# Attention and two MLPs on one core: two token chunks share a pass of the MLPs, and the weights' spill is taken out

## The chip, the cores and the metric

The kernel runs on one core of a Trainium2 chip. The metric is the device time of one execution in microseconds (us); lower is better. TensorE (PE) multiplies, VectorE (DVE), ScalarE (ACT) and GpSimd (POOL) do the elementwise work, and SyncE (SP) issues every transfer.

## What is computed

The reference, cut to what matters. Attention over 2 batches, 8 heads, 576 positions and 64 dimensions a head, with a bias from relative positions that a small MLP makes, is followed by two MLPs over the 1152 tokens (512 to 2048 to 512): the first with ELU, the second with softplus.

```python
def _attn_ref(q, k, v, w1, b1, w2):
    scores = scale * np.matmul(q, k.transpose(0, 1, 3, 2))
    psi_rel = np.log1p(np.abs(rel))
    psi_i = np.log1p(np.maximum(pos[:, None], 1.0))
    h = np.maximum((psi_rel / psi_i)[..., None] @ w1 + b1, 0.0)
    scores = scores + (h @ w2).transpose(2, 0, 1)[None]
    attn = np.exp(scores - np.max(scores, axis=-1, keepdims=True))
    attn = attn / (np.sum(attn, axis=-1, keepdims=True) + 1e-09)
    return np.matmul(attn, v)

def _moe_ref(x, w_in, w_out):
    h = x @ w_in
    return np.where(h > 0.0, h, np.exp(np.minimum(h, 0.0)) - 1.0) @ w_out

def _moe2_ref(x, w_in, w_out):
    h = x @ w_in
    return (np.maximum(h, 0.0) + np.log1p(np.exp(-np.abs(h)))) @ w_out
```

## The kernel before

Everything is computed in split precision: an operand is a high part and a low part, and a product is three matmuls (high by high, high by low, low by high).

**Attention.** The queries stand in blocks (`BLOCKS`), the first of 64 rows of both batches together, the others of 128 rows; a unit is a block, a batch and a pair of heads, 36 in all. Ahead of a block its bias is made in stages of 16 rows (`bias_y`, `bias_mm`, `bias_ev`, `bias_out`): four `y` tiles on VectorE or GpSimd, two half-stages of 12 matmuls into `pb`, an eviction of each by ScalarE into `sg`, and a transfer that lays the rows out by head. A unit then has `scores` on TensorE, `soft` on VectorE (bias added, row maximum taken: `e` and `mx`), `expo` on ScalarE, `turn` (nine groups of four transposes for four units), `e_hi` and `e_lo` (tile `et`), and `av`, 30 matmuls with V. Four units end in 128 finished tokens (`fin_x`, `fin_t`, `fin_hi`, `fin_lo`), split into `xh` and `xl`, which the MLPs read. Before all this V needs a power-of-two scale from its largest entry: `v_bound` on ScalarE, `v_max` on VectorE, then `all_max` over the partitions (a diagonal by VectorE, a matmul with ones, a reduction by VectorE), in one piece.

**MLPs.** Tokens stand in chunks of 512, 256 and 384 (`CHS`). A weight tile `f`, of 16, has 128 of the 2048 hidden columns. For chunk `c` and tile `f` of layer `m`, `ffn1` forms the first product in one PSUM bank (12 matmuls), ScalarE and VectorE apply the activation (two or three ScalarE passes, then `both` on VectorE, the last that reads the bank), `hi` and `lo` split it into `g`, and `drain` multiplies by the second weights into accumulators that stay in four banks. Four banks hold first products. A chunk goes through all 16 tiles before the next begins, in the order of `ORDER`: 0, 1, 2 in the first layer and 0, 2, 1 in the second.

**Weights.** They arrive as 64-bit floats, in 64 halves of tiles (32 for each layer), and are built into 32-bit words on the core: a load of 512 KB (`dma`), a first pass on ScalarE (`abs`), a clamp on VectorE or GpSimd and three integer steps on VectorE (`bits`), then `split_hi` on ScalarE and `split_lo` on VectorE. The words of the first layer are made during the attention and the first MLP pass, written to device memory (`spill`) and read back ahead of their use (`reload`). Those of the second layer are made when their place in SBUF comes free.

**Order.** Every step is a task with an engine, a cost and a due time (`DUE`, `LEAD`); the class `Order` forms a list of each engine's instructions from them when the program is built, eight rounds forward and backward. Each engine then works in that order. Where the list has TensorE idle before the first `av`, `idle` puts warm-up matmuls on the identity into the gap:

```python
    def idle(at, gap):
        if not pas:
            warm(min(int(gap * 0.92 / 0.094), 60))
```

and 34 stand at the very start.

Of the kernel before, what the change touches and what calls it, by code (L numbers as in the profile page):

```python
# [27 lines left out]
CHS = [512, 256, 384]  # L28

ORDER = [(0, 1, 2), (0, 2, 1)]  # L30
# [18 lines left out]
NRAW, NWB, NRL = 2, 3, 3  # L49
# [5 lines left out]
    BY=-9.79, BMM=-1.13, BEV=-3.13, BOUT=15.84, VD=-7.95, VB=-11.68, VHI=1.98, VLO=33.24, VS=-9.83, VZ=-10.22,  # L55
    KH=12.0, KL=1.05, KB=5.39, QH=-0.25, QL=8.6, QD=14.51, SC=3.22, SO=-22.46, EX=2.92, EH=7.47, EL=-6.03,
    TR=-8.2, AV=5.84, FS=3.18, FX=16.16, FT=-19.73, FH=5.97, FL=12.76, TAB=18.07, WD=11.76, WA=4.33, WS=-6.11,
    WB=-4.29, RL=-1.33, WL1=7.35, AC=-5.72, GH=17.01, GL=-21.01, DR=-22.41, DH=11.55, FI=6.5, R1=0.61, R2=-1.7,
    WI=19.2, F1=56.11,
)  # L60
LEAD = [-1.26, 21.84, 8.41, 24.57, -1.58]
# [50 lines left out]
class Weights:  # L112
# [76 lines left out]
def attention(xctx, tc, qe, qt, kt, vt, par, tab, xh, xl, W, M):  # L189
# [82 lines left out]
    warm(34)  # L272
# [80 lines left out]
    def idle(at, gap):  # L353

        if not pas:
            warm(min(int(gap * 0.92 / 0.094), 60))
# [300 lines left out]
    vsx = add(V, 2.2, lambda e: (all_max(vg, vm[:, 0:1]), v_scale()), [vmx], -0.5)  # L657
# [128 lines left out]
    def weights(i, x):  # L786
# [3 lines left out]
        di = DUE["WD"] + DUE["WI"] * (2 * i + x) if m == 0 else dj - DUE["WL1"]  # L790
# [20 lines left out]
    def tile_of(j):  # L811
# [3 lines left out]
        if c == ORDER[m][0]:  # L815
# [19 lines left out]
        half = 2 * n <= 512  # L835
        if not half or f % 2 == 0:
            r_g.append(([hi], []))
        else:
            hi.order.append(t_hi[seq[j - 1]])
        g_use = r_g[-1][1]  # L840
        t_hi[t] = hi
# [235 lines left out]
class Mlps:  # L1077


    def __init__(self, ctx, tc, xh, xl, W, out):  # L1080
        self.ctx, self.tc, self.nc, self.xh, self.xl, self.W, self.out = ctx, tc, tc.nc, xh, xl, W, out
        self.gt, self.outs = [], {}

        self.ps4 = ctx.enter_context(tc.tile_pool(name="ps4", bufs=1, space=PSUM)).tile([P, 4, 512], F32, name="ps4")
        self.acc = [self.ps4[:, n] for n in range(4)]

    def open(self):
        self.ap = self.ctx.enter_context(self.tc.tile_pool(name="ap", bufs=2, side="right"))
        self.W.open_early()
# [158 lines left out]
```

## Time and profile before

| | us |
|---|---|
| median of three runs | 638.02 |
| lowest and highest | 634.76, 638.15 |
| the profiled execution | 637.52 |
| its span, first to last instruction | 635.7 |
| TensorE busy (5427 matmuls) | 610.2 |
| VectorE, ScalarE, GpSimd busy | 432.2, 406.8, 129.6 |
| granted TensorE clock, mean | 0.985 |

The busy time of TensorE counts matmuls that overlap, so it is an upper bound. The other rows are averages over three stages with different limits: a start of some 56 us, the attention up to about 220 us, and the MLPs. A line number in a row is that of the program printed above; a row's names are the program's, with buffer numbers left out. In the trace a group of instructions in a row stands as one line, with its count behind the x.

### The profile page before, as it was taken

The numbers are of one execution on the slowest core, as the hardware profiler recorded it, in microseconds if no ns is written. First come the engines' busy times: TensorE is split into PE (matmuls) and PEld (weight loads), VectorE is DVE, ScalarE is ACT, GpSimd is POOL, SyncE is SP. The second block draws the span as 40 slices with busy tenths as digits, with TensorE's granted clock in tenths as the row PEclk, the third lists the DMA queues.
The fourth block names the chain that finished last, engine by engine and source line by source line (L and its number), as shares of the span: only waits on it lengthen the run. The fifth ranks groups of instructions, "written<-read, shape, count | busy, mean of one in ns | idle before, by whom it ended". The sixth has DMA issues, their size and how long they took to land.

```text
span 635.7 us, 13697 instructions
## 1 busy us (share of the span) xinstructions
PE 610.2 (96%) x5427; PEld 520.8 (82%) x5427; DVE 432.2 (68%) x857; ACT 406.8 (64%) x831; POOL 129.6 (20%) x172
## 2 busy tenths in 40 slices
PE   6889989898999999999999999999999999999996
PEld 5667767676777888888899999998888889988985
DVE  4669888898799998887742248879788732223322
ACT  3644779899899985665553345659577554445652
POOL 5212768876661000000000001110010100000000
PEclk8879999999899999999999999999999999999999
DMA  8625454646254377887400003333333210000000
GB/s 329 208 84 163 138 149 143 189 137 166 72 157 155 88 208 236 269 254 222 157 27 1 1 0 100 122 121 123 125 108 114 86 47 20 1 1 18 34 1 33
DMA packets 28288, 73.21 MB, mean 115 GB/s; under 512 B 3136, under 2 KB 3520, under 8 KB 27968
## 3 DMA queue, kind: packets, MB, share of 16 engines
q1 hardware_dynamic: 28224, 72.34, 36.7%
q8 instruction: 42, 0.69, 0.5%
q14 instruction: 22, 0.18, 0.1%
HBM read 49.79 MB, written 10.75 MB: 95 GB/s over the span
## 4 chain that ended last, share of the span: by engine, by line
PE 84%; DVE 5%; ACT 4%; DMA 3%; POOL 1%; issue 1%; DVEq 0%; POOLq 0%; ACTq 0%
PE ps L1158 32%; PE ph L1118 31%; PE warm L270 6%; PE pb L387 4%; PE tp L550 4%; PE ps L510 4%; PE pa L575 3%; DMA bias<-sg 2%; ACT e L537 1%; DVE e L520 1%; ACT sg L399 1%; POOL y L378 1%; DVE et L559 1%; ACT et L554 1%; DMA sp<-sg 1%
## 5 line engine op out<-in xcount | busy, mean ns | idle before, releaser
L1118 PE MATMUL ph<-xh,wh 128*128 128x512 f32 (+2 forms) x384 | 130.0, 338 | 0.7 <-DVE t L1134 0.7
L1118 PE MATMUL ph<-xl,wh 128*128 128x512 f32 (+2 forms) x384 | 129.5, 337 | 0.0
L1118 PE MATMUL ph<-xh,wl 128*128 128x512 f32 (+2 forms) x384 | 129.5, 337 | 0.0
L378 POOL TENSOR_SCALAR y<-tpk,nbp 128x576 f32<-128x576 f32 x108 | 90.7, 855 | 57.0 <-PE pb L387 54.3
L1158 PE MATMUL ps<-g,wh 128*128 128x512 f32 (+2 forms) x384 | 96.3, 338 | 0.0
L1158 PE MATMUL ps<-wh,g 128*128 128x512 f32 x288 | 92.1, 393 | 0.0
L154 POOL TENSOR_SCALAR w<-w 128x512 f32<-128x512 f32 x38 | 25.2, 663 | 299.6 <-ACT w L146 267.3
L1143 DVE TENSOR_TENSOR g<-t,g 128x512 fp32r<-128x512 f32 (+2 forms) x96 | 52.5, 555 | 39.4 <-ACT g L1140 37.4
L1118 PEld LDWEIGHTS ph<-xh,wh 128*128 128x128 f32 x384 | 72.3, 188 | 6.6 <-DVE t L1134 0.8
L1140 ACT CAST g<-t 128x512 fp32r<-128x512 f32 (+2 forms) x96 | 48.0, 508 | 46.3 <-PE ps L1158 35.4
L1118 PEld LDWEIGHTS ph<-xl,wh 128*128 128x128 f32 x384 | 72.5, 189 | 5.7
L1118 PEld LDWEIGHTS ph<-xh,wl 128*128 128x128 f32 x384 | 72.2, 188 | 5.5
L1158 PEld LDWEIGHTS ps<-g,wh 128*128 128x128 f32 x384 | 67.0, 188 | 5.4
L1136 DVE SCALAR_TENSOR_TENSOR t<-ph,t 128x512 f32<-128x512 f32 (+2 forms) x48 | 26.7, 557 | 61.6 <-ACT t L1130 61.6
L1158 PE MATMUL ps<-g,wl 128*128 128x512 f32 (+2 forms) x192 | 64.6, 336 | 0.0
L1158 PEld LDWEIGHTS ps<-wh,g 128*128 128x128 f32 x288 | 54.1, 188 | 12.1
L399 ACT ACTIVATE sg<-pb,bcst,inv 128x288 f32<-128x288 f32 x72 | 42.5, 590 | 30.8 <-PE pb L387 27.6
L559 DVE SCALAR_TENSOR_TENSOR et<-tp,et 128x512 f16<-128x512 f32 x81 | 53.8, 682 | 6.2 <-ACT et L554 6.1
L1158 PE MATMUL ps<-wl,g 128*128 128x512 f32 x144 | 56.7, 394 | 0.0
L146 ACT ACTIVATE w<-r 128x512 f32<-128x512 f32 x64 | 42.7, 669 | 21.6 <-DMA r<-in_wb_dram 10.7
L537 ACT ACTIVATE e<-e,mx 128x576 f32<-128x576 f32 x72 | 55.6, 774 | 1.4 <-DVE mx L520 1.4
L550 PE MATMUL tp<-ident,e 128*128 128x128 f32 x324 | 49.7, 284 | 4.4 <-DVE xl L615 2.9
(116 smaller groups left out, 1069.6 us busy)
## 6 DMA issues: line engine op xcount, KB each, us to landing
r<-in_wa_dram SPq DMA_DIRECT2D x32, 512.0 KB, 4.3
r<-in_wb_dram SPq DMA_DIRECT2D x32, 512.0 KB, 3.6
bias<-sg SPq DMA_DIRECT2D x32, 288.0 KB, 3.4
wd<-w SPq DMA_DIRECT2D x32, 256.0 KB, 4.5
rl<-wd SPq DMA_DIRECT2D x32, 256.0 KB, 4.3
kr<-in_kt_dram SPq DMA_DIRECT2D x4, 576.0 KB, 6.7
vr<-in_vt_dram SPq DMA_DIRECT2D x2, 1152.0 KB, 10.6
sp<-sg SPq DMA_DIRECT2D x8, 288.0 KB, 3.4
```

The costliest lines, as they stand in the source:

```text
L146: self.nc.scalar.activation(w.bitcast(F32), self.raws[i, x][:, :, 1].bitcast(F32), AF.Abs)
L270: nc.tensor.matmul(wdst, wi[:, :P], wi[:, : 512 - SH], start=True, stop=True)
L378: eng.tensor_scalar(y, tpk[:, b0 : b0 + S], BIG, nbp[:, qd : qd + 1], op0=ALU.min, op1=ALU.max)
L399: nc.scalar.activation(sgs[bi, s][:, n * SH : (n + 1) * SH], pbs.pop((bi, s, n)), AF.Identity, bias=bcst, scale=inv[:, col : col + 1])
L537: nc.scalar.activation(e, e, AF.Exp, bias=mxs[u][:, x : x + 1], scale=-1.0, accum_out=sums[u - hp][:, h : h + 1])
L550: nc.tensor.transpose(tp[:, r], e[:, t * P : (t + 1) * P], ident)
L559: nc.vector.scalar_tensor_tensor(et[:, 1], tp, 2.0**14, et[:, 0], op0=ALU.mult, op1=ALU.subtract)
L1118: nc.tensor.matmul(ps, a[:, kk], x[:, kk], start=n == 0, stop=n == 3 * KT - 1)
L1136: nc.vector.scalar_tensor_tensor(t[0], ps, 0.0, t[0], op0=ALU.max, op1=ALU.add)
L1140: nc.scalar.copy(g[0], t[0])
L1143: nc.vector.tensor_sub(g[1], t[0], g[0])
L1158: self.nc.tensor.matmul(o, a, x, start=f == 0 and n == 0, stop=f == FT - 1 and n == 2)
```

## The change

1. `ORDER` is replaced by `PASSES`: chunks 0 and 1, 768 tokens, go through the weight tiles together, and chunk 2 follows. In the first layer chunk 1 trails by four tiles (`LAG`). A weight tile so serves 768 tokens in the first pass.
2. Chunk 1 has accumulators of its own in two banks (`ps2`), so two banks hold first products, one on each side. In the first layer two 256-column accumulators share a bank, which a matmul with a zero tile opens. The `g` tiles of chunk 1 are a pair of buffers of their own.
3. `spill` and `reload` are gone. The weights of the first layer go from load to split in one run, like those of the second; there are three buffers for raw words and four for words, instead of two, three and three for reloads.
4. `all_max` gives way after the diagonal and after the matmul, so that other instructions can stand between; the scale of V becomes three tasks.
5. Warm-ups: 22 at the very start instead of 34; in a gap half of what is left after 1 us, at most 20. The program has 101 instead of 357.
6. The due times and the choice of engine for each `y` tile, clamp and cast are new, so every engine's order changes.

```diff
-ORDER = [(0, 1, 2), (0, 2, 1)]
+PASSES = [(0, 1), (2,)]
+
+LAG = [4, 0]
...
-NRAW, NWB, NRL = 2, 3, 3
+NRAW, NWB = 3, 4
...
-    WI=19.2, F1=56.11,
+    WB=4.81, WL1=14.9, AC=1.55, GH=8.27, GL=-8.52, DR=9.09, FI=-0.31, R1=-0.34, R2=0.5, F1=32.77,
...
-    def spill(self, i, x):
-        self.nc.sync.dma_start(self.dram[i][x], self.words.pop((i, x)))
-
-    def reload(self, i, x):
-        w = self.words[i, x] = self.rl.tile([P, DM], F32, tag="rl", name=f"rl{i}{x}")
-        self.nc.sync.dma_start(w, self.dram[i][x])
...
-    warm(34)
+    warm(22)
...
         nc.vector.tensor_scalar_mul(dg, ident, src)
+        yield
         pm = pst.tile([P, 512], F32, tag="pt", name=f"pm_{dst.name}")[:, :P]
         nc.tensor.matmul(pm, ones, dg, start=True, stop=True)
+        yield
         nc.vector.tensor_reduce(dst, pm, axis=mybir.AxisListType.X, op=ALU.max)
...
-            warm(min(int(gap * 0.92 / 0.094), 60))
+            warm(min(int(max(gap - 1.0, 0.0) * 0.5 / 0.094), 20))
...
-    vsx = add(V, 2.2, lambda e: (all_max(vg, vm[:, 0:1]), v_scale()), [vmx], -0.5)
+    vsx = add(V, 0.29, lambda e: next(vmax), [vmx], -1)
+    vsx = vmm = add(T, 0.5, lambda e: next(vmax), [vsx], -1)
+    vsx = add(V, 1.0, lambda e: v_scale(), [vsx], -1)
+    r_pt.append(([vmm], [vsx]))
...
-    seq = [(m, c, f) for m in range(2) for c in ORDER[m] for f in range(FT)]
+    seq = []
+    for m in range(2):
+        for cs in PASSES:
+            for f in range(FT + LAG[m] * (len(cs) - 1)):
+                seq += [(m, c, f - LAG[m] * i) for i, c in enumerate(cs) if 0 <= f - LAG[m] * i < FT]
...
-        if m == 0:
-            sp = add(D_, 1.2, lambda e: W.spill(i, x), [a], di + DUE["WB"], lat=2.4)
-            r_word.append(([a0], [sp]))
-            a = rl = add(D_, 1.0, lambda e: W.reload(i, x), [sp, t_w], dj - DUE["RL"], lat=1.8)
...
+        self.zero = self.ap.tile([P, P], F32R, name="zero", bufs=1)
...
-        self.left = self.ctx.enter_context(self.tc.tile_pool(name="phleft", bufs=3, space=PSUM))
+        self.left = self.ctx.enter_context(self.tc.tile_pool(name="phleft", bufs=1, space=PSUM))
+        self.ps2 = self.left.tile([P, 2, 512], F32, name="ps2")
...
-        return 0 if j < NE else (j - NE + 1) % 4
+        return 0 if j < NE else (j - NE + 1) % 2
+
+    def acc(self, m, c, k):
+
+        if c != 1:
+            return self.ps4[:, k, : CHS[c] if m == 0 else DM]
+        return self.ps2[:, k // 2, k % 2 * CHS[c] :][:, : CHS[c]] if m == 0 else self.ps2[:, k]
...
+        tag, n, bufs = ("gs", CHS[1], 2) if c == 1 else ("g", 512, 3)
+        return [self.ap.tile([P, n], F32R, tag=f"{tag}{x}", name=f"g{x}{m}{c}{f}", bufs=bufs)[:, : CHS[c]] for x in range(2)]
...
+            two = m == 0 and c == 1
+            if two and f == 0 and j % 2 == 0:
+                self.nc.tensor.matmul(self.ps2[:, j // 2], self.zero, self.xh[0][:, 0], start=True, stop=False)
```

VectorE at the maximum of V. Before; `dg_vg` is the diagonal, `pm_vg` the result of the matmul, `vg` the maximum:

```order
L453 TENSOR_TENSOR vm<-vm 128x2
L454 TENSOR_TENSOR vm<-vm 128x1
L435 TENSOR_TENSOR q_522<-qr_0_248,q_521 128x256
L287 TENSOR_SCALAR dg_vg_535<-ident,vm 128x128
L290 TENSOR_REDUCE vg<-pm_vg_537 128x1
L276 TENSOR_SCALAR e_244<-vg 128x1
```

After:

```order
L448 TENSOR_TENSOR vm<-vm 128x2
L449 TENSOR_TENSOR vm<-vm 128x1
L430 TENSOR_TENSOR q_396<-qr_0_202,q_395 128x256
L277 TENSOR_SCALAR dg_vg_411<-ident,vm 128x128
L430 TENSOR_TENSOR q_403<-qr_1_205,q_402 128x256 x2
L151 TENSOR_SCALAR w_409<-w_409 128x512
L282 TENSOR_REDUCE vg<-pm_vg_436 128x1
L266 TENSOR_SCALAR e_198<-vg 128x1
```

Between the diagonal and the reduction now stand two subtractions of q parts and the clamp of a weight half.

VectorE in the attention, in the third and fourth block. Before; lines 156 to 160 are the integer steps on a weight half `w` from the raw words `r`, `e` and `mx` the softmax pass, `et` the low part of the transposed exponentials:

```order
L615 TENSOR_TENSOR xl_1010<-pr_4104,xh_1009 128x4x128
L559 SCALAR_TENSOR_TENSOR et_4_4136<-tp_4_4116,et_4_4136 128x512
L156 TENSOR_SCALAR w_3886<-w_3886 128x512
L435 TENSOR_TENSOR q_4102<-qr_1_3456,q_4101 128x256
L158 SCALAR_TENSOR_TENSOR w_3886<-r_3775,w_3886 128x512
L586 TENSOR_SCALAR sm_3794<-sm_3794 128x8
L160 SCALAR_TENSOR_TENSOR w_3886<-r_3775,w_3886 128x512
L559 SCALAR_TENSOR_TENSOR et_5_4204<-tp_5_4159,et_5_4204 128x512
L559 SCALAR_TENSOR_TENSOR et_6_4207<-tp_6_4166,et_6_4207 128x512
L520 ISA e_4261,mx_4260<-ps_98,bias_3335 128x576
L520 ISA mx_4260 128x1
```

After, at the corresponding place:

```order
L587 RECIPROCAL sm_3004<-sm_3004 128x8
L430 TENSOR_TENSOR q_3321<-qr_0_2737,q_3320 128x256
L518 ISA e_3592,mx_3591<-ps_64,bias_2123 128x576
L518 ISA mx_3591 128x1
L518 ISA e_3592,mx_3591<-ps_64,bias_2123 128x576
L518 ISA mx_3591 128x1
L557 SCALAR_TENSOR_TENSOR et_0_3594<-tp_0_3577,et_0_3594 128x512
L557 SCALAR_TENSOR_TENSOR et_1_3610<-tp_1_3584,et_1_3610 128x512
L591 SCALAR_TENSOR_TENSOR xs_3695<-pa_3404,xsc,sm_3004 128x512
L557 SCALAR_TENSOR_TENSOR et_2_3709<-tp_2_3697,et_2_3709 128x512
L557 SCALAR_TENSOR_TENSOR et_3_3724<-tp_3_3704,et_3_3724 128x512
```

The weight steps no longer stand between the passes of the attention.

VectorE in the first layer's first pass of the MLPs. Before; `t` and `g` are a tile's activation and its low part, `wl` a weight's low part from the reloaded words `rl`:

```order
L1143 TENSOR_TENSOR g_5619<-t_5591,g_5618 128x512
L154 TENSOR_SCALAR w_5625<-w_5625 128x512
L156 TENSOR_SCALAR w_5625<-w_5625 128x512
L158 SCALAR_TENSOR_TENSOR w_5625<-r_5577,w_5625 128x512
L160 SCALAR_TENSOR_TENSOR w_5625<-r_5577,w_5625 128x512
L1134 SCALAR_TENSOR_TENSOR t_5642<-t_5642,ph_5600 128x512
L1143 TENSOR_TENSOR g_5667<-t_5642,g_5666 128x512
L1134 SCALAR_TENSOR_TENSOR t_5671<-t_5671,ph_5629 128x512
L154 TENSOR_SCALAR w_5675<-w_5675 128x512
L156 TENSOR_SCALAR w_5675<-w_5675 128x512
L186 TENSOR_TENSOR wl_5615<-rl_5647,wh_5614 128x512
L1143 TENSOR_TENSOR g_5694<-t_5671,g_5693 128x512
```

After:

```order
L1132 SCALAR_TENSOR_TENSOR t_5073<-t_5073,ph_5029 128x512
L1141 TENSOR_TENSOR g_5047<-t_5021,g_5046 128x256
L157 SCALAR_TENSOR_TENSOR w_5042<-r_4971,w_5042 128x512
L155 SCALAR_TENSOR_TENSOR w_5056<-r_5003,w_5056 128x512
L1132 SCALAR_TENSOR_TENSOR t_5097<-t_5097,ph_5059 128x256
L157 SCALAR_TENSOR_TENSOR w_5056<-r_5003,w_5056 128x512
L1141 TENSOR_TENSOR g_5094<-t_5073,g_5093 128x512
L176 TENSOR_TENSOR wl_4974<-w_4944,wh_4973 128x512
L176 TENSOR_TENSOR wl_5123<-w_5056,wh_5122 128x512
L176 TENSOR_TENSOR wl_5053<-w_5042,wh_5052 128x512
L153 TENSOR_SCALAR w_5127<-w_5127 128x512
L1132 SCALAR_TENSOR_TENSOR t_5144<-t_5144,ph_5105 128x512
```

Passes of 512 and of 256 tokens alternate, and the weight steps stand between them.

## Rows read from the trace of the kernel before

**Rows 1.** Windows: length; busy us PE, PEld, DVE, ACT, POOL; clock; DMA; GB/s.

```profile
0.00:56.00 56.00, 46.15 (x461) 36.89 (x461) 36.72 (x84) 26.18 (x43) 15.56 (x26) 0.88 0.61 204
56.00:88.00 32.00, 30.80 (x613) 22.56 (x610) 27.79 (x53) 21.50 (x45) 19.61 (x23) 1.00 0.50 147
88.00:220.00 132.00, 123.26 (x2057) 95.85 (x2052) 120.37 (x263) 122.13 (x271) 78.25 (x100) 0.99 0.48 138
220.00:632.00 412.00, 409.96 (x2308) 365.46 (x2306) 246.92 (x460) 237.02 (x474) 16.19 (x24) 1.00 0.30 93
```

**Rows 2.** The page, part 4: the chain of waits, shares by line.

```profile
PE ps L1158 32%; PE ph L1118 31%; PE warm L270 6%; PE pb L387 4%; PE tp L550 4%; PE ps L510 4%; PE pa L575 3%; DMA bias<-sg 2%; ACT e L537 1%; DVE e L520 1%; ACT sg L399 1%; POOL y L378 1%; DVE et L559 1%; ACT et L554 1%; DMA sp<-sg 1%
```

**Rows 3.** The chain in order of time (start, length, what): DMA.

```profile
82.22 4.79 DMA sp<-sg
...
115.23 5.78 DMA bias<-sg
```

**Rows 4.** The same: matmul groups of attention and MLPs.

```profile
101.29 1.02 PE tp L550 x8
...
106.46 0.87 PE pa L575 x30
...
241.41 2.75 PE ph L1118 x12
...
274.38 2.80 PE ph L1118 x12
...
333.63 1.43 PE ph L1118 x12
```

**Rows 5.** Timeline of TensorE (start, length, what, idle before), first 44 us.

```profile
15.01 2.42 PE L270 MATMUL warm<-ident 128*128 128x224 f16 x12
...
34.52 0.80 PE L289 MATMUL pm_vg<-dg_vg,ones 128*128 128x128 f32 x2 [4.91 <-DVE dg_vg L287]
...
35.10 8.22 PE L270 MATMUL warm<-ident 128*128 128x224 f16 x60
...
43.26 0.44 PE L387 MATMUL pb<-y,w2h 128*32 128x288 f16 x8
```

**Rows 6.** Timeline of VectorE, first 57 us.

```profile
32.64 1.81 DVE L287 TENSOR_SCALAR dg_vg<-ident,vm 128x128 f32<-128x128 f32 x1
...
35.35 0.29 DVE L290 TENSOR_REDUCE vg<-pm_vg 128x1 f32<-128x128 f32 x1 [0.89 <-PE pm_vg L289]
...
43.85 1.81 DVE L380 TENSOR_SCALAR y<-tpk,nbp 128x576 f32<-128x576 f32 x4 [4.99 <-PE pb L387]
...
55.90 0.74 DVE L520 CUSTOM_DVE_ANT_0 e<-ps,bias 128x576 f32<-128x576 f32 x1
```

**Rows 7.** A 4 us window, columns as in rows 1.

```profile
36.00:40.00 4.00, 4.00 (x24) 3.27 (x23) 2.79 (x10) 3.44 (x5) 0.00 (x0) 0.52 0.27 73
```

**Rows 8.** Groups by shape: busy us, mean ns, idle before, releasers.

```profile
L156 DVE TENSOR_SCALAR w<-w 128x512 int32<-128x512 int32 x64 | 27.6, 432 | 9.2 <-POOL w L154 8.5
...
L158 DVE SCALAR_TENSOR_TENSOR w<-r,w 128x512 int32<-128x512 int32 x64 | 45.0, 703 | 1.1
...
L160 DVE SCALAR_TENSOR_TENSOR w<-r,w 128x512 int32<-128x512 int32 x64 | 46.6, 729 | 0.9
...
L146 ACT ACTIVATE w<-r 128x512 f32<-128x512 f32 x64 | 42.7, 669 | 21.6 <-DMA r<-in_wb_dram 10.7 <-DMA r<-in_wa_dram 10.6 <-DMA bias<-sg 0.3
...
L1125 ACT ACTIVATE t<-ph 128x512 f32<-128x512 f32 x16 | 9.6, 597 | 16.2 <-PE ph L1118 16.1
...
L1126 ACT ACTIVATE t<-t 128x512 f32<-128x512 f32 x16 | 10.1, 633 | 0.5
...
L1134 DVE SCALAR_TENSOR_TENSOR t<-t,ph 128x512 f32<-128x512 f32 x16 | 11.0, 685 | 4.6 <-ACT t L1126 4.5
```

**Rows 9.** Timeline of VectorE, two weight steps back to back.

```profile
220.39 0.68 DVE L186 TENSOR_TENSOR wl<-rl,wh 128x512 fp32r<-128x512 f32 x1
220.99 0.68 DVE L158 SCALAR_TENSOR_TENSOR w<-r,w 128x512 int32<-128x512 int32 x1
```

More of the change, by code (lines that the diff above doesn't have):

```diff
@@ L789, in weights @@
         dj = DUE["F1"] + w_first[m, f] + 0.4 * x
-        di = DUE["WD"] + DUE["WI"] * (2 * i + x) if m == 0 else dj - DUE["WL1"]
+        di = dj - DUE["WL1" if m else "WL0"]
         dw = add(D_, 1.9, lambda e: W.dma(i, x), [], di, lat=1.4)
@@ L834, in tile_of @@
         r_t.append(([ac], [hi, lo]))
[L835 to L841, printed above, removed]
         dr = t_dr[t] = add(
             T, 12 * (n / 2400 + 0.0155) if m == 0 else n / P * 3 * 0.231, lambda e: M.drain((m, c, f), made.pop(j)[4]), [hi, lo] + t_wp[m, f][1],
-            d + DUE["DH" if half else "DR"] * w,
+            d + DUE["DR"],
         )
-        g_use.append(dr)
+        r_gs[c == 1].append(([hi], [dr]))
         if j:
@@ L851, in tile_of @@
         if f == 0:
-            dr.after += t_acc
+            dr.after += t_acc[c == 1]
         if f == FT - 1:
-            t_acc.clear()
             fins = []
@@ L1081, in __init__ @@
         self.ctx, self.tc, self.nc, self.xh, self.xl, self.W, self.out = ctx, tc, tc.nc, xh, xl, W, out
-        self.gt, self.outs = [], {}
+        self.outs = {}
         self.ps4 = ctx.enter_context(tc.tile_pool(name="ps4", bufs=1, space=PSUM)).tile([P, 4, 512], F32, name="ps4")
-        self.acc = [self.ps4[:, n] for n in range(4)]
     def open(self):
         self.ap = self.ctx.enter_context(self.tc.tile_pool(name="ap", bufs=2, side="right"))
+        self.zero = self.ap.tile([P, P], F32R, name="zero", bufs=1)
+        nc = self.nc
+        nc.gpsimd.tensor_scalar(self.zero, self.xh[0][:, 0, :P].bitcast(F32), 0.0, 0.0, op0=ALU.mult, op1=ALU.mult)
         self.W.open_early()
@@ L1098, in slot @@
     def slot(self, j):
-        return 0 if j < NE else (j - NE + 1) % 4
+        return 0 if j < NE else (j - NE + 1) % 2
[3 more added lines that the diff above has]
+        return self.ps2[:, k // 2, k % 2 * CHS[c] :][:, : CHS[c]] if m == 0 else self.ps2[:, k]
     def g_tiles(self, m, c, f):
-        half = f % 2 if 2 * CHS[c] <= 512 else 0
-        if not half:
-            self.gt = [self.ap.tile([P, 512], F32R, tag=f"g{x}", name=f"g{x}{m}{c}{f}", bufs=3) for x in range(2)]
-        return [t[:, half * CHS[c] : (half + 1) * CHS[c]] for t in self.gt]
+        tag, n, bufs = ("gs", CHS[1], 2) if c == 1 else ("g", 512, 3)
+        return [self.ap.tile([P, n], F32R, tag=f"{tag}{x}", name=f"g{x}{m}{c}{f}", bufs=bufs)[:, : CHS[c]] for x in range(2)]
     def ffn1(self, m, c, f, slot):
@@ L1153, in drain @@
             if m == 0:
-                prods = [(self.acc[j][:, : CHS[c]], a[:, js], x) for a, x in ((h, gh), (h, gl), (l, gh))]
+                prods = [(a[:, js], x) for a, x in ((h, gh), (h, gl), (l, gh))]
             else:
-                prods = [(self.acc[j], a[:, js], x) for a, x in ((gh, h), (gh, l), (gl, h))]
-            for n, (o, a, x) in enumerate(prods):
-                self.nc.tensor.matmul(o, a, x, start=f == 0 and n == 0, stop=f == FT - 1 and n == 2)
+                prods = [(a[:, js], x) for a, x in ((gh, h), (gh, l), (gl, h))]
+            two = m == 0 and c == 1
+            if two and f == 0 and j % 2 == 0:
+                self.nc.tensor.matmul(self.ps2[:, j // 2], self.zero, self.xh[0][:, 0], start=True, stop=False)
+            for n, (a, x) in enumerate(prods):
+                self.nc.tensor.matmul(
+                    self.acc(m, c, j), a, x, start=f == 0 and n == 0 and not two, stop=f == FT - 1 and n == 2 and not (two and j % 2 == 0)
+                )
     def finish_hi(self, c, k):
-        self.nc.scalar.copy(self.xh[c][:, k], self.acc[k][:, : CHS[c]])
+        self.nc.scalar.copy(self.xh[c][:, k], self.acc(0, c, k))
     def finish_lo(self, c, k):
-        self.nc.vector.tensor_sub(self.xl[c][:, k], self.acc[k][:, : CHS[c]], self.xh[c][:, k])
+        self.nc.vector.tensor_sub(self.xl[c][:, k], self.acc(0, c, k), self.xh[c][:, k])
     def out_half(self, c, k, x):
@@ L1170, in out_half @@
         if x == 0:
-            self.nc.scalar.copy(o[:, sl], self.acc[k][:, sl])
+            self.nc.scalar.copy(o[:, sl], self.acc(1, c, k)[:, sl])
         else:
-            self.nc.vector.tensor_copy(o[:, sl], self.acc[k][:, sl])
+            self.nc.vector.tensor_copy(o[:, sl], self.acc(1, c, k)[:, sl])
     def out_dma(self, c, k):
```

54 lines of the change are left out of this document (27 added, 27 removed).

## The prediction, made before the changed kernel was run

> **What bounds the kernel now.** I read the stages first. From 220 us to 632 us TensorE is busy for 410 of 412 us, while VectorE and ScalarE have 247 and 237 [rows 1]. That is the two MLPs, and there only fewer matmul columns would help; the change keeps the columns. So what can be won lies before 220 us, and what can be lost lies in the MLPs becoming less dense. In the 132 us before 220, TensorE shows 123, VectorE 120 and ScalarE 122 us [rows 1]: three engines at over 90%, none alone the bound. In the first 56 us VectorE is busy for only 37 [rows 1]. The chain of waits puts 6% of the span, about 38 us, on warm-up matmuls [rows 2], more than on any single step of the attention. All of them stand before the first attention times V product, so nearly the whole start is blamed on matmuls whose results nobody reads. Last I looked for transfers on the chain: three waits like the two of 4.8 and 5.8 us shown, each for the last bias rows of a new query block [rows 3].
>
> **The profiled time.** Its span is 635.7 us, its time 637.5; the median of the three runs is 638.0. I sum against 637.5 and take 638.0 as its equal. Under 0.5%, some 3 us, a measurement can't be told from no change.
>
> **The start, up to the first softmax pass on VectorE, at 55.9 us [rows 6].** Three edits act here. (1) The cross-partition maximum of V is taken apart. Before, VectorE ran the diagonal (1.81 us from 32.64), then stood 0.9 us for the matmul and reduced at 35.35 [rows 6]; now a subtraction and a weight step fill that wait. This saves 0.9 us at most. (2) Sixty warm-ups stood behind that matmul and took 8.22 us, so the bias matmuls that follow began at 43.26 [rows 5], and VectorE stood idle for 4.99 us until they had freed its y buffers [rows 6]. Now 20 stand there. At the same 0.137 us each they take 2.7 us, which is 5.5 us less; the idle time goes, since its y work comes 5.5 us sooner than it waited. The planner asked for those sixty because it assumed 0.094 us for each. (3) Of the first 14 y tiles VectorE now makes all, before seven; four take it 1.81 us [rows 6]. And the 12 warm-ups that held the second half of bias stage 0 back from 15.01 to 17.4 [rows 5] no longer stand there. VectorE's own work up to the first softmax pass keeps its size (84 instructions before, 85 now), so what is won is idle time, of which there are 56 minus 37, or 19 us [rows 1]. About 5 us are bound to the loads and to the first chain and stay. Of the other 14 I take 10: the 5.0 and 0.9 above, and 4 of the first 30 us. The bounds: 13 us if every wait goes, 2 us if the clock (below) eats the rest.
>
> **The weights leave the attention.** By the built order VectorE had, between the first softmax pass and the first MLP tile, 2 clamps, 14, 13 and 13 of the three integer steps and 8 low-part subtractions; now 5, 4, 4, 4 and 3. That is 10 × 0.432 + 9 × 0.703 + 9 × 0.729 + 5 × 0.68 − 3 × 0.44 = 19.3 us of durations [rows 8, 9] (the clamp taken like the first step). Two steps in a row start 0.60 apart where each lasts 0.68 [rows 9], so it is 19.3 × 0.88 = 17 us of engine time. Against it stand 7 more y tiles, 7 × 0.45 = 3.2 us [rows 6], and 7 more q parts, about 2.5 us as an estimate from the same rows. VectorE is 11 us lighter for the same attention. ScalarE loses 9 of 13 first passes (0.669 each [rows 8]), 4 of 9 casts and 4 q casts, together about 9 us. Besides, the first MLP tile now stands some 3 us of TensorE's attention work earlier (five groups of 30 V products and 36 transposes follow it, before four and 20: 0.87 + 16 × 0.127 = 2.9 us [rows 4]); that only moves. TensorE itself loses warm-ups between 56 and 70 us and nothing else. Where three engines are equally full, the least relieved sets the gain: ScalarE's 9 us plus 2 of the moved work is my 11. The bounds: 3 us, if TensorE is the true bound there and only the moved work counts; 16, if the spills' and weights' transfers were also what made the bias waits 4.8 and 5.8 us [rows 3]. The spill and reload, 64 issues on SP, lie beside other work; I cost them at nothing else. The 32 loads of 512 KB of the first layer move with the weights: eight go before the last bias rows, the others in the first MLP pass, 1 MB for each 8.5 us of TensorE, or some 120 GB/s where the start had 204 [rows 1]. GpSimd's clamps now stand behind its last y tile and wait for nothing there.
>
> **The MLPs.** The matmul columns are the same; two zero matmuls of 512 columns are added (under 0.5 us). What the first pass costs VectorE: a weight tile now serves 512 + 256 tokens, so TensorE spends 2 × 2.80 + 2 × 1.43 = 8.5 us on it [rows 4]. VectorE needs for it two halves of 0.432 + 0.703 + 0.729 + 0.68 and two passes of 0.685 for the 512 tokens, some 0.42 each for the 256: (5.09 + 2.2) × 0.88 = 6.4 us [rows 8, 9], three quarters of TensorE's time. Before, a tile served 512 tokens in 5.6 us, for which VectorE would need (5.09 + 1.37) × 0.88 = 5.7: without work done ahead and spilled it could not keep up. With a cover of 8.5 us it can. What gets tighter is PSUM: the second chunk's accumulators take two banks, so two banks instead of four hold first products. A bank of 512 tokens is held for 0.597 + 0.633 on ScalarE and 0.685 on VectorE, 1.9 us plus hand-overs [rows 8], and between two uses stand a drain and a 256-token tile, 2.80 + 1.43 = 4.2 us [rows 4]. That leaves some 2 us for queueing; behind a first product that waits for its bank stand the drains, which have nothing to wait for, so a wait there is lost. I take 3 us of stalls for both layers, most of them among the first five tiles, where transposes, weight steps and MLP passes share VectorE; bounds 0 and 22. The 2.9 us of attention moved behind the first tile come back here. The last chunk is now 384 tokens, three output blocks to copy out instead of two: 0.4 us, between 0 and one VectorE pass of 0.74 [rows 6].
>
> **Sum.** 637.5 − 10 − 11 + 2.9 + 3 + 0.4 = 622.8, so 623 us.
>
> **Rivals.** (a) The clock. In the window from 36 to 40 us the granted clock was 0.52, that is mostly 1.2 GHz, after TensorE had stood idle for 4.91 us before the maximum's matmul at 34.52; from 56 us on it was 1.00 [rows 1, 5, 7]. With 101 warm-ups instead of 357 the start may run at 1.2 GHz throughout. A bias half-stage takes 0.44 us for eight of its twelve matmuls at 2.4 GHz [rows 5], some 0.5 in all, and would take 0.5 more; nine of them before the first softmax pass and some seven after it make 8 us, and the time would be 631. Against it: VectorE, not TensorE, is the fuller one there once the warm-ups go. The Trainium skill (TensorE: Matmul & The Clock Gate, What's actually happening) says that the throttled clock is the default and that activity releases it, which speaks against cutting warm-ups; by it the sum would be this rival's. The 0.52 agrees with it; that the start depends on it is not shown by any row.
> (b) The MLPs are no longer dense, and the kernel is slower. The place is the pass of chunks 0 and 1 in the first layer: VectorE works in order, so each weight step queued ahead of a tile's pass holds its PSUM bank 0.60 us longer [rows 9]. From 4.2 us of holding time on, TensorE waits. One step too many in each of the pass's 32 tiles is 32 × 0.6 = 19 us, so 642; with the second layer too it would be over 660. For it: two banks and a full queue. Against it: a quarter of VectorE's time is free there.
> (c) TensorE's own order bounds the attention, and only the moved 3 us come: 637.5 − 10 − 3 + 6.3 = 631.
> (d) The bias transfers were the hidden bound and everything falls into place: 637.5 − 13 − 16 + 2.9 = 611. Matmul groups of 512 columns took 2.75 to 2.80 us [rows 4] with no cause that I can name; where buffers now lie may move that by some 3 us either way, so 608.
>
> **Chances.** Forecast (615 to 629) 0.52, (a) 0.09, (b) 0.14, (c) 0.11, (d) 0.08, and 0.06 for a mere draw of gains and stalls. The range of 609 to 640 takes in (a), (c), most of (d) and the first part of (b). Faster by over 0.5%: 0.52 + 0.09 + 0.11 + 0.08 = 0.80. Within it: the draw and a little of (b), 0.08. Slower: 0.12.
>
> **What would show it.** Right: the first softmax pass near 46 us; VectorE idle for less than 12 us before it; the first MLP tile near 199 us; TensorE again over 99% busy from there, with at most a few us of waits on the t passes. The start is wrong if that softmax pass comes after 52 us at a clock near 0.5. The attention step is wrong if the distance between it and the first MLP tile stays near 164 us. The MLP step is wrong if TensorE's groups wait on VectorE's passes in the 135 us after the first tile, or if the groups of 512 columns leave 2.7 to 2.8 us.

## The result, and the profile after

The changed kernel takes 620.96 us (median of four runs, 620.69 to 621.39) against 638.09 before in the same comparison: a ratio of 0.9745, 95% interval 0.9712 to 0.9777. In a later comparison with more runs (below, after_again) it was 620.55 against 635.31, ratio 0.9775 (0.9751 to 0.9799). The forecast was 623. The kernel before ran between 633 and 638 us, and its trace is of a run near the top of that; so the two traces differ by 17.0 us (spans of 635.7 and 618.7) where the medians of the later comparison differ by 14.8. A stage's difference in the traces can be off by 2 us or so.

From here a line number is that of the kernel shown. In the changed kernel `warm` is line 260, the diagonal 277, the reduction 282, `y` 373 (GpSimd) and 375 (VectorE), `pb` 382, the softmax pass 518, first products 1116, drains 1160.

The stages of the changed kernel, columns as in [rows 1], the last two rows with windows that end or begin at the first softmax pass and at the first MLP tile:

```profile
0.00:56.00 56.00, 38.04 (x359) 23.86 (x361) 48.02 (x101) 33.38 (x58) 18.91 (x28) 0.76 0.68 227
56.00:88.00 32.00, 28.93 (x588) 21.03 (x586) 28.88 (x60) 24.94 (x55) 19.18 (x23) 1.00 0.38 109
88.00:220.00 132.00, 129.66 (x2069) 103.50 (x2066) 118.79 (x259) 117.17 (x258) 57.80 (x78) 1.00 0.26 75
220.00:618.00 398.00, 392.07 (x2168) 349.08 (x2165) 242.38 (x453) 232.15 (x462) 29.97 (x35) 1.00 0.23 76
...
0.00:45.78 45.78, 29.08 (x260) 18.37 (x261) 39.88 (x85) 27.01 (x45) 16.24 (x24) 0.78 0.70 237
...
45.78:197.02 151.24, 144.90 (x2561) 111.50 (x2561) 132.84 (x290) 132.54 (x295) 76.91 (x100) 0.98 0.30 85
```

The third row takes in 23 us of the MLPs, since the first MLP tile now starts at 197.0. VectorE now works 48 of the first 56 us, where it had 37 [rows 1]. Up to its first softmax pass it is idle for 45.78 - 39.88 = 5.9 us; before it was 55.90 - 36.62 = 19.3:

```profile
0.00:55.90 55.90, 46.05 (x460) 36.81 (x461) 36.62 (x84) 26.18 (x43) 15.56 (x26) 0.88 0.61 204
```

The timeline of VectorE in the changed kernel, columns as in [rows 6]:

```profile
27.77 0.39 DVE L277 TENSOR_SCALAR dg_vg<-ident,vm 128x128 f32<-128x128 f32 x1
27.97 1.66 DVE L430 TENSOR_TENSOR q<-qr,q 128x256 fp32r<-128x256 f32 x2
29.55 0.41 DVE L151 TENSOR_SCALAR w<-w 128x512 f32<-128x512 f32 x1
29.88 0.28 DVE L282 TENSOR_REDUCE vg<-pm_vg 128x1 f32<-128x128 f32 x1
...
45.78 0.74 DVE L518 CUSTOM_DVE_ANT_0 e<-ps,bias 128x576 f32<-128x576 f32 x1
```

No idle time stands before the reduction, where 0.89 us stood [rows 6]. TensorE at the same place, as in [rows 5]:

```profile
22.97 2.09 PE L260 MATMUL warm<-ident 128*128 128x224 f16 x20
28.21 0.49 PE L280 MATMUL pm_vg<-dg_vg,ones 128*128 128x128 f32 x2 [3.15 <-DVE dg_vg L277]
28.54 3.63 PE L260 MATMUL warm<-ident 128*128 128x224 f16 x20
34.52 0.44 PE L382 MATMUL pb<-y,w2h 128*32 128x288 f16 x8 [2.36 <-ACT sg L394]
```

Behind the maximum the bias matmuls wait for ScalarE's eviction and no longer for warm-ups. The page's chain by line, which had warm-ups with 6% [rows 2], has none among those it lists:

```profile
PE ps L1160 32%; PE ph L1116 31%; PE pb L382 5%; PE tp L548 5%; PE pa L573 4%; PE ps L508 4%; DVE e L518 2%; ACT sg L394 2%; DVE et L557 2%; DMA kr<-in_kt_dram 1%; ACT e L535 1%; DVE y L375 1%; ACT vh L440 1%; ACT vh L482 1%; DVE xl L1168 1
```

All of TensorE's waits from the first MLP tile on (197 to 613 us; us in total, times, longest):

```profile
PE ps L1160 <- DVE g L1141: 0.5, 1, 0.5
PE ps L1160 <- DVE xl L1168: 0.4, 1, 0.4
PE tp L548 <- DVE et L557: 0.3, 1, 0.3
```

Not one is for a `t` pass, the wait by which a bank comes back. By stage, from trace to trace:

| | before | after | difference | forecast |
|---|---|---|---|---|
| first softmax pass at | 55.9 | 45.8 | -10.1 | -10 |
| from there to the first MLP tile | 163.8 | 151.2 | -12.6 | -11 |
| from there to the start of the last matmul | 410.6 | 415.5 | +5.0 | +5.9 |
| tail | 5.4 | 6.1 | +0.7 | +0.4 |

### The profile page after: what moved, and what is told of

It reads as the page before. It is cut to its first block, busy times and chain, and to the rows that moved or that the text cites. A ratio compares the mean times of both kernels' runs of the same rounds, so it can differ in the third digit from the quotient of the medians.

```text
span 618.7 us, 13017 instructions
## 1 busy us (share of the span) xinstructions
PE 588.7 (95%) x5173; PEld 497.5 (80%) x5173; DVE 438.1 (71%) x869; ACT 407.6 (66%) x830; POOL 125.9 (20%) x162
## 4 chain that ended last, share of the span: by engine, by line
PE 81%; DVE 7%; ACT 6%; issue 2%; DMA 2%; SPq 1%; POOL 0%; DVEq 0%; ACTq 0%; POOLq 0%
PE ps L1160 32%; PE ph L1116 31%; PE pb L382 5%; PE tp L548 5%; PE pa L573 4%; PE ps L508 4%; DVE e L518 2%; ACT sg L394 2%; DVE et L557 2%; DMA kr<-in_kt_dram 1%; ACT e L535 1%; DVE y L375 1%; ACT vh L440 1%; ACT vh L482 1%; DVE xl L1168 1%
## 5 line engine op out<-in xcount | busy, mean ns | idle before, releaser
L1138 ACT CAST g<-t 128x256 fp32r<-128x256 f32 (+2 forms) x96 | 49.1, 512 | 83.1 <-PE ps L1160 76.4
L1160 PE MATMUL ps<-g,wh 128*128 128x256 f32 (+2 forms) x384 | 97.0, 339 | 0.5 <-DVE g L1141 0.5
L1160 PE MATMUL ps<-wh,g 128*128 128x512 f32 x288 | 95.1, 394 | 0.4 <-DVE xl L1168 0.4
L1141 DVE TENSOR_TENSOR g<-t,g 128x256 fp32r<-128x256 f32 (+2 forms) x96 | 54.2, 565 | 52.6 <-ACT g L1138 52.0
L373 POOL TENSOR_SCALAR y<-tpk,nbp 128x576 f32<-128x576 f32 x95 | 74.2, 795 | 60.9 <-PE pb L382 46.6
L151 POOL TENSOR_SCALAR w<-w 128x512 f32<-128x512 f32 x38 | 32.0, 841 | 216.7 <-ACT w L143 146.0
L394 ACT ACTIVATE sg<-pb,bcst,inv 128x288 f32<-128x288 f32 x72 | 42.5, 591 | 22.2 <-PE pb L382 14.5
L382 PE MATMUL pb<-y,w2h 128*32 128x288 f16 x576 | 37.3, 313 | 16.2 <-ACT sg L394 10.0
L552 ACT ACTIVATE et<-tp 128x512 f16<-128x512 f32 x81 | 46.3, 596 | 5.0 <-PE tp L548 5.0
## 6 DMA issues: line engine op xcount, KB each, us to landing
vr<-in_vt_dram SPq DMA_DIRECT2D x2, 1152.0 KB, 10.7
```

Source lines behind the costliest of these rows:

```text
L151: eng.tensor_scalar(wf, wf, F64_HUGE, F64_TINY, op0=ALU.min, op1=ALU.max)
L373: eng.tensor_scalar(y, tpk[:, b0 : b0 + S], BIG, nbp[:, qd : qd + 1], op0=ALU.min, op1=ALU.max)
L382: nc.tensor.matmul(pb[32 * c : 32 * c + 32], w, ys[bi, s, c][:, n * SH : (n + 1) * SH, half], start=ps == 0, stop=ps == 2,)
L394: nc.scalar.activation(sgs[bi, s][:, n * SH : (n + 1) * SH], pbs.pop((bi, s, n)), AF.Identity, bias=bcst, scale=inv[:, col : col + 1])
L552: nc.scalar.activation(et[:, 0], tps[g, k].rearrange("p t i -> p (t i)"), AF.Copy, scale=2.0**14)
L1138: nc.scalar.copy(g[0], t[0])
```

## The experiments

Where an edit leaves the planner's input alone, every engine keeps its order, but for the warm-ups or the steps that are edited; two_banks alone forms a new order. Ratios are to the kernel before on the same chip.

**Warm-ups.** few_warm is the kernel before with the new rule, old_warm the changed kernel with the old one, no_warm the changed kernel with none.

```diff
-    warm(34)
+    warm(22)
...
-            warm(min(int(gap * 0.92 / 0.094), 60))
+            warm(min(int(max(gap - 1.0, 0.0) * 0.5 / 0.094), 20))
```

> The kernel before with the new rule for warm-ups alone (22 at the very start, half of the gap less 1 us, at most 20); all else stands in the same order on every engine. My theory (VectorE's waits behind the warm-ups are what is won): the first softmax pass moves from 55.9 us to about 50.5 and the time falls by 5 us, to 633. Rival (the clock stays at 1.2 GHz and eats it): the first softmax pass comes at 54 us or later and the time stays within 1.5 us of 638.

> The changed kernel with the old rule for warm-ups (34 at the very start, 0.92 of the gap, at most 60); all else in the same order. My theory: the first softmax pass moves from 45.8 us to 50 or 51, the time rises by 5 us to 626. Rival (fewer warm-ups cost clock that the old rule would give back): the time is 621 or less, with the granted clock above 0.9 between 36 and 52 us, where the changed kernel has 0.50.

> The changed kernel without a single warm-up matmul; all else in the same order. My theory (VectorE, not TensorE, is the fuller engine of the start): the clock is near 0.5 for most of the first 50 us, and the time is within 2 us of 621. Rival (the clock decides the start): the bias matmuls and the first scores at half speed move the first softmax pass to 50 us or later, and the time is 625 or more.

few_warm: 628.14 us, 0.9895 (0.9862 to 0.9927), so 6.7 us less; the first softmax pass at 48.1 us, 7.8 earlier (its trace has the first MLP tile another 4.0 earlier, more than the ratio leaves room for; it is of the fastest of its four runs, 625.67 us, and the trace of the kernel before is of one near the top of its runs). old_warm: 619.27 us, 0.9759 (0.9735 to 0.9783), first softmax pass at 45.6. no_warm: 621.26 us, 0.9795 (0.9765 to 0.9825), first softmax pass at 45.6. On one chip no_warm is 2.0 us slower than old_warm, and their runs lie apart (620.76 to 622.32, and 618.73 to 619.44).

What VectorE's `y` work waited for its buffers in the first 60 us, of before, few_warm, the changed kernel and old_warm in this order:

```profile
DVE y L380 <- PE pb L387: 11.6, 3, 5.0
...
DVE y L380 <- PE pb L387: 5.2, 4, 3.2
...
DVE y L375 <- PE pb L382: 2.3, 4, 0.9
...
DVE y L375 <- PE pb L382: 0.8, 2, 0.5
```

So in the old order the warm-ups cost what I said, and somewhat more. TensorE in few_warm at the maximum:

```profile
30.51 0.80 PE L289 MATMUL pm_vg<-dg_vg,ones 128*128 128x128 f32 x2 [5.83 <-DVE dg_vg L287]
31.09 3.94 PE L270 MATMUL warm<-ident 128*128 128x224 f16 x20
```

The maximum's matmul comes 4.0 us earlier than at 34.52 [rows 5], and the softmax pass follows 3.8 us sooner behind it. In the new order the warm-ups cost nothing: for old_warm I had expected 626 us, and the rival's "621 or less" came. TensorE in old_warm:

```profile
22.88 5.92 PE L260 MATMUL warm<-ident 128*128 128x224 f16 x60
28.64 0.40 PE L280 MATMUL pm_vg<-dg_vg,ones 128*128 128x128 f32 x2
28.87 4.86 PE L260 MATMUL warm<-ident 128*128 128x224 f16 x49
34.25 0.44 PE L382 MATMUL pb<-y,w2h 128*32 128x288 f16 x8 [0.52 <-ACT sg L394]
```

The sixty take 5.92 us, 0.099 each, next to the planner's 0.094; behind the next 49 the bias matmul still waits for ScalarE. In the kernel before, sixty took 8.22 [rows 5], after TensorE had stood idle for 4.91 us. They ran at two clocks, the first 4.7 us at 0.50 and the rest at 1.00:

```profile
35.10:39.84 4.74, 4.74 (x27) 3.87 (x26) 3.37 (x12) 3.27 (x5) 0.00 (x0) 0.50 0.19 55
39.84:43.30 3.46, 3.46 (x40) 3.28 (x42) 0.00 (x0) 0.51 (x1) 0.00 (x0) 1.00 0.46 152
```

So the planner's figure fits the full clock and not the other, and the prediction's 0.137 us each is a mean over both. The twenty behind the maximum in the changed kernel took 3.63 us, 0.18 each, where I had 2.7. The clock from 36 to 52 us, of old_warm and of the changed kernel:

```profile
36.00:52.00 16.00, 15.84 (x219) 11.85 (x221) 15.43 (x27) 9.71 (x18) 3.57 (x4) 1.00 0.59 168
...
36.00:52.00 16.00, 12.29 (x113) 5.26 (x114) 14.08 (x27) 8.79 (x16) 2.15 (x3) 0.50 0.53 150
```

The changed kernel does run at 1.2 GHz there, as rival (a) had it, and VectorE, with 14 of 16 us the fuller engine, reaches its softmax pass all the same. The Trainium skill says that the throttled clock is the default and that activity releases it (TensorE: Matmul & The Clock Gate, What's actually happening). These two rows agree: 1.00 with TensorE busy for 15.84 of 16 us, 0.50 with it busy for 12.29. That the time follows the clock, they do not show.

**The changed kernel beside old_warm, on one chip:**

> The changed kernel itself, for a comparison with the next run on the same chip: a ratio to the kernel before of 0.974 to 0.980. One theory has it 1 to 2 us behind the same kernel with the old rule for warm-ups, whose first softmax pass came no later and whose attention was 1.5 us shorter at a granted clock of 1.00; the other has the two alike to within 0.5 us.

> The changed kernel with the old rule for warm-ups, once more. Theory that the warm-ups cost nothing in the new order, and that the clock they hold gives a little back: 1 to 2 us less than the changed kernel. Rival (the two differ by the chip or the call only): within 0.5 us of it.

after_again: 620.55 us (619.48 to 621.54), 0.9775 (0.9751 to 0.9799). old_warm_again: 619.28 us (618.66 to 619.69), 0.9754 (0.9731 to 0.9776). With the old rule, the warm-ups' own time included, the kernel is 1.3 us shorter, about 0.2%; the intervals overlap, but old_warm gave 619.3 in both comparisons. It is the fastest version that computes everything, by a margin at the edge of what can be told.

**The weights in the attention.** Three edits of the kernel before, all on the halves begun ahead of the first MLP tile. no_prep leaves them out (and few_warm_no_prep does so with the new rule for warm-ups); no_transfers leaves out their loads and spills alone; thin_steps keeps ScalarE's passes and the transfers and cuts VectorE's steps. The cores of no_prep, no_transfers and thin_steps:

```diff
     def dma(self, i, x):
         m, f = self.wq[i]
+        if self.early_:
+            self.gone.add((i, x))
+            return
...
         w, nc = self.words[i, x], self.nc
+        if (i, x) in self.gone:
+            return
```

```diff
+        if self.early_:
+            self.gone.add((i, x))
+            if self.one is not None:
+                self.raws[i, x] = self.one
+                return
...
-        self.nc.sync.dma_start(self.dram[i][x], self.words.pop((i, x)))
+        if (i, x) not in self.gone:
+            self.nc.sync.dma_start(self.dram[i][x], self.words.pop((i, x)))
```

```diff
+        if self.thin and (n or eng is nc.vector):
+            w, wf, low, high = (t[:, :8] for t in (w, wf, low, high))
```

> The kernel before with the weight halves that are begun ahead of the first MLP tile left out: no load, first pass, clamp, integer step or spill of them, and their later reading takes other numbers of the same size (so the MLPs work on wrong weights). Everything else keeps its order. My theory (the least relieved of three full engines, ScalarE, sets the gain): the distance from the first softmax pass to the first MLP tile falls from 164 us by 7 to 10 us, the time to 628 to 631. Rival (TensorE's own order is the bound): by less than 3 us, 635 or more. Rival (the transfers were the bound): by 13 us or more, 625 or less.

> The kernel before with both edits at once: the new rule for warm-ups, and no preparation of the weight halves that are begun ahead of the first MLP tile (their later reading takes other numbers, so the MLPs work on wrong weights). Alone the first gave a ratio of 0.9895 and the second 0.9898. Theory that the two lie in different stages and add: a ratio of 0.979, some 621 to 624 us, with the first MLP tile near 201 us. Rival (both take up the same slack of VectorE in the attention): a ratio of 0.985 or more, some 626 us, with the first MLP tile at 205 us or later.

> The kernel before without the 512 KB loads and the spills of the weight halves that are begun ahead of the first MLP tile, but with all their work on ScalarE, VectorE and GpSimd (on the numbers of the first half loaded, so the MLPs work on wrong weights). My theory (the work on the engines, not the transfers, holds up the attention): the distance from the first softmax pass to the first MLP tile stays within 2 us of 164. Rival (the weights' transfers are what make the bias transfers late): it falls by 4 us or more, and the no_prep run's 7 us are mostly that.

> The kernel before with VectorE's steps (the three integer steps, and its clamps) on the weight halves made ahead of the first MLP tile cut to 8 of 512 columns; ScalarE's passes, GpSimd's clamps, loads, spills and the order stay (the MLPs work on wrong weights). VectorE loses some 14 us of engine time in the attention, ScalarE and the transfers nothing. My theory (the least relieved of the full engines sets the gain): the distance from the first softmax pass to the first MLP tile falls by less than 2 us. Rival (VectorE alone is the bound): by 5 us or more, as much as in the no_prep run.

no_prep: 627.77 us, 0.9898 (0.9873 to 0.9924), 6.5 us less. few_warm_no_prep: 619.49 us, 0.9762 (0.9733 to 0.9792), first MLP tile at 200.9. no_transfers: 632.55 us, 0.9968 (0.9949 to 0.9986). thin_steps: 635.23 us, 0.9993 (0.9971 to 1.0014). The stretch from the first softmax pass to the first MLP tile, of before, no_prep, no_transfers and thin_steps (columns as in [rows 1]):

```profile
55.90:219.65 163.75, 153.81 (x2662) 118.18 (x2659) 147.91 (x315) 143.28 (x314) 97.87 (x122) 0.99 0.49 140
...
53.36:210.30 156.94, 151.23 (x2662) 116.90 (x2659) 127.99 (x276) 136.37 (x301) 82.28 (x110) 1.00 0.30 83
...
54.56:214.40 159.84, 152.28 (x2662) 117.06 (x2660) 148.85 (x315) 142.63 (x314) 97.69 (x122) 1.00 0.29 81
...
57.24:219.20 161.96, 153.97 (x2662) 119.78 (x2660) 135.15 (x315) 142.43 (x314) 89.85 (x122) 0.98 0.48 140
```

thin_steps takes 12.8 us from VectorE and the stretch loses 1.8, the time nothing: VectorE alone was not the bound. no_prep takes 19.9 us from VectorE and 6.9 from ScalarE and the stretch loses 6.8, as much as ScalarE. But no_transfers, with both engines as busy as before, already loses 3.9 in the trace and 2.0 by the ratio, so the transfers (loads and spills together) were not free as I had them. No run took ScalarE's passes alone; how the rest splits between it and the two together stays open. Warm-ups and weights do not take up the same slack: they give 6.7 and 6.5 us apart and 15.1 together. That is 1.9 more than the sum, and better than the 0.979 expected; the intervals, some 2 us either way, leave room for it.

**How near the MLPs are to the edge.** The changed kernel with one integer step done twice, or four times; and the kernel before with two banks.

```diff
-            nc.vector.scalar_tensor_tensor(w, low, 29, w, op0=ALU.logical_shift_right, op1=ALU.bitwise_or)
+            for _ in range(self.more):
+                nc.vector.scalar_tensor_tensor(w, low, 29, w, op0=ALU.logical_shift_right, op1=ALU.bitwise_or)
```

```diff
-        return 0 if j < NE else (j - NE + 1) % 4
+        return 0 if j < NE else (j - NE + 1) % 2
```

> The changed kernel with one integer step of each first-layer weight half done twice on VectorE from the first MLP tile on (some 28 halves x 0.60 us = 17 us more of VectorE's time; the numbers stay the same). My theory (a quarter of VectorE's time is free in the first pass and the two banks carry the rest): no change to within 2 us, 620 to 623. Rival (each step queued ahead of a tile's pass holds one of two banks longer and TensorE waits): 10 us or more, 631 or more.

> The same with that step done four times, some 28 x 1.8 = 50 us more of VectorE's time. Between 240 and 331 us VectorE has 18 us free, and it is full up to 240. My theory (what counts is VectorE's free time in the first pass): TensorE waits for what exceeds it, about 20 to 30 us, 641 to 651. Rival (the later stages take the work up, since the tiles are made ahead): under 626.

> The kernel before with two PSUM banks for first products from the sixth tile on, instead of four (the list of each engine is formed anew for it). My theory (with a tile's words read back and no integer steps due, a bank is back well before its next use): within 2 us of the kernel before, TensorE over 99% busy in the MLPs. Rival (two banks are too few by themselves): 5 us or more, with TensorE waiting on the t passes.

one_more: 641.39 us, 1.0111 (1.0081 to 1.0142), so 20.8 us over the changed kernel's 620.55 (on another chip; 21.3 by the two ratios). three_more: 702.87 us, 1.1076 (1.1047 to 1.1104), 82 over it. two_banks: 641.39 us, 1.0100 (1.0077 to 1.0123), 6.1 over the kernel before. In none of the three did my theory hold. VectorE's load in the first pass, of the changed kernel and of one_more:

```profile
197.00:240.00 43.00, 42.66 (x348) 35.76 (x347) 41.60 (x79) 29.34 (x56) 6.06 (x9) 1.00 0.36 121
240.00:290.00 50.00, 50.00 (x283) 43.48 (x283) 46.14 (x88) 35.49 (x69) 8.77 (x9) 1.00 0.42 140
290.00:335.00 45.00, 45.00 (x277) 40.12 (x276) 27.99 (x53) 20.36 (x42) 3.56 (x4) 1.00 0.32 106
...
240.00:290.00 50.00, 46.41 (x255) 39.26 (x253) 49.55 (x91) 33.33 (x64) 6.54 (x8) 1.00 0.39 126
```

VectorE's free time lies late: 5.3 us of the first 93, in which it builds 24 weight halves, and 17 of the last 45, in which it builds eight. The step that one_more adds fills the rest from 240 to 290 us (49.55 of 50), and from its first MLP tile on TensorE waits for a `t` pass twelve times, 12.5 us in all. That sum, one of these waits (on a first product of 512 tokens), and the same sum in three_more:

```profile
PE ph L1119 <- DVE t L1135: 12.5, 12, 2.1
...
261.43 0.50 PE L1119 MATMUL ph<-xh,wh 128*128 128x512 f32 x1 [0.91 <-DVE t L1135]
...
PE ph L1119 <- DVE t L1135: 47.5, 19, 6.3
```

By the start of chunk 2 one_more is 14.5 us late (349.7 against 335.2), by that of the second layer 20.4. The step was also doubled for the second-layer halves that are made in the first layer: VectorE ran it 106 times, not 64. At 0.60 us a step that is 25 us more of VectorE's time for 21 us of the kernel's; in three_more it is 190 times, 76 us more, for 82 us, where I had expected 20 to 30 (its mean granted clock also falls, to 0.943). So what is added to VectorE there comes back nearly whole. In two_banks TensorE waits for few `t` passes from its first MLP tile on:

```profile
PE ph L1118 <- DVE t L1134: 2.2, 2, 1.7
PE tp L550 <- DVE et L559: 0.8, 1, 0.8
PE ph L1118 <- DVE t L1136: 0.4, 1, 0.4
PE ps L1158 <- DVE o L1173: 0.3, 1, 0.3
```

From its first tile to its last matmul it takes 416.4 us, 5.8 more than the kernel before. The waits come to 3.7 us, where the kernel before had 0.7; where the other 2.8 lie I did not follow. Its order is a new one, so the 1% is that of two banks and the order made for them.

## Why the prediction held, point by point

**The start.** VectorE was the engine to look at, but that -10 was right to 0.1 us is luck. VectorE's idle time ahead of the pass fell by 13.4 us (19.3 to 5.9), as much as I had "if every wait goes", and its busy time, which I had keep its size, grew by 3.3 (36.6 to 39.9): it makes 25 `y` tiles there instead of 19, and some small instructions run long (a `w2e` of 128 by 32 takes 3.23 us, 0.24 before). The working had 5.0 for the sixty warm-ups, 0.9 for the maximum and 4 for the first 30 us. In the old order the new rule alone moves the pass by 7.8 us, 3.8 of it behind the maximum. What I did not see is that the edit I called the largest is not needed: in the new order the old rule gives the same start, so the new order with the split of the maximum and the new `y` engines brings the 10 us by itself. What of it is due to which was not tried. few_warm_no_prep, at 46.6, does not tell: it has no weight work in the start, where the changed kernel's VectorE does seven clamps and integer steps ahead of the pass and the kernel before six.

**Rival (a), the clock.** The clock was at 0.50 from 36 to 52 us and cost 1.3 us (2.0 without any warm-ups), not 8: VectorE was the fuller engine, the reason given against it. A bias half-stage at that clock takes 0.84 us (36.70 to 37.54 in the changed kernel) and 0.50 at the full one (34.52 to 35.02), so it was priced at 0.5 where 0.34 is lost.

**The weights out of the attention.** 11 against 12.6. The moved work was 2.0 us, not 2.9: TensorE's matmuls of the attention after the first tile's start take 9.3 us, 7.3 before. ScalarE was relieved by 10.7 us (143.28 to 132.54), where I had 9, and with the 2.0 that comes near the 12.6. The least relieved engine as the measure stood the test that it had (thin_steps), but it is not the whole account: in no_transfers no engine was relieved and the stretch fell all the same. "I cost them at nothing else", of the spill and reload, was wrong by up to the 2 us of no_transfers. Rival (c), TensorE's own order, fell with no_prep. But TensorE is now nearly full between 88 us and the first MLP tile; the changed kernel and the kernel before:

```profile
88.00:197.02 109.02, 107.02 (x1882) 84.98 (x1879) 95.81 (x215) 101.23 (x229) 55.07 (x75) 1.00 0.25 69
...
88.00:219.65 131.65, 122.91 (x2056) 95.54 (x2050) 120.02 (x262) 121.78 (x270) 78.25 (x100) 0.99 0.48 138
```

**The MLPs.** +5.9 against +5.0: the 2.0 moved, 0.5 for the two zero matmuls, 0.9 in first products and 1.6 in drains (each matmul from its start to the next one's, waits included; the waits are 1.2 us, before 0.7). The 3 us of stalls on banks did not come. The sum was nearly right, and the reason for it was not. "A quarter of VectorE's time is free there" was 16% over the pass, and 6% in its first two thirds. Rival (b) was priced at one step too many, 19 us, and the kernel stands right before that point: one more step a half cost 20.8 us, where I expected nothing. Two banks, which I thought enough by 2 us, cost the kernel before 1% with the order made for them.

**The rest.** The tail was 0.7 instead of 0.4. (d) didn't come: start and attention each stayed short of its bound.

**What the gain is made of.** Fewer warm-ups and no early weights give the kernel before 15.1 us; the change as a whole gives 14.3 by the later ratio and 16.3 by the first. Leaving the early weights out is a bound, since their work is then nowhere. In the new order fewer warm-ups have no part in the gain: with the old rule it is 1.3 us larger. As I read it, that a weight tile serves 768 tokens brings nothing by itself, and lets the weight work stand under TensorE's for 5 us; a version with the weights made late and 512 tokens a tile was not tried.

## What to carry to other kernels

Free time is counted where the work will stand, in windows no longer than the buffers let it run ahead; a mean over a pass hid that VectorE was full in the part that mattered. When three engines are equally full, relief of one may bring nothing, as VectorE's 12.8 us did here; count what the least relieved loses, and then the transfers. Filler work ordered from a planned gap is harmless where the plan holds, and costs time where an engine behind it needs the result of what follows. A stage that comes out to 0.1 us is still taken apart: here less idle time and more work cancelled.

## What the runs showed of the hardware that was not expected

The 2.72 and 2.80 us of a group of twelve 512-column matmuls go by the weight tile. The first layer of two_banks shows it best, from its chain in order of time; the rows are the first products of tiles 6 and 7:

```profile
256.94 2.72 PE ph L1118 x12
...
262.39 2.80 PE ph L1118 x12
```

In the kernel before and after, in both layers, tiles 4 to 6 run mostly at 2.72 to 2.76 and tiles 7 to 15 at 2.80; groups of 384 columns take mostly 2.08 to 2.11 and then 2.12, with the same border. Tiles 0 to 6 lie in the pools `wfirst` and `wearly` on one side of SBUF, 7 to 15 in `wrest` on the other. That the place is the cause was not tried.

At the very start the granted clock reads 1.00, yet the first warm-ups of the changed kernel take 4.02 us for 22, 0.183 each, almost twice the 0.099 above:

```profile
1.35 4.02 PE L260 MATMUL warm<-ident 128*128 128x224 f16 x22 [1.35 <-POOL ident masks.py:199]
...
0.00:4.00 4.00, 2.65 (x15) 2.10 (x16) 0.47 (x3) 1.49 (x2) 1.61 (x9) 1.00 0.54 161
```

All but the last few start 0.187 us apart, the last ones 0.097; the change comes at 4.9 us, and the trace's own record of the clock begins at 5.0. In no_warm that record begins at 19.2 us, and ahead of it the same eight score matmuls take 1.16 us under a column of 1.00; the changed kernel's take 0.69 where its clock is on record as 1.00 (from 18.6 us on):

```profile
17.57 1.16 PE L508 MATMUL ps<-k,xl 64*128 64x288 f32 x8
...
8.00:20.00 12.00, 7.04 (x60) 4.28 (x61) 11.59 (x20) 5.93 (x12) 6.71 (x6) 1.00 1.02 417
...
18.64 0.69 PE L508 MATMUL ps<-k,xl 64*128 64x288 f32 x8
```

So up to the first record the durations tell the clock, and its column, which stands at 1.00 there, does not; the clocks of windows that begin at 0 read too high.
